# Three PSUM pools instead of two in a fused attention-and-gate kernel: own banks for attention and for the gate

## The chip, the cores and the metric

The kernel runs on one core of a Trainium2 chip. The metric is the device time of one execution in microseconds (us), lower is better. A profile is one execution taken with the hardware profiler; all times inside it are counted from the start of its span. Engines are named as the profile names them: PE (TensorE matmul), PEld (its weight load), DVE (VectorE), ACT (ScalarE), POOL (GpSimd), SP (SyncE).

On one core a run is called slow when it took over 1.5% more than the fastest run of the same kernel.

## The reference, cut to what matters

Eight batches (B = 8) of eight heads, 576 positions, head size 64. First an attention with 32 landmarks, whose middle factor is a 32 x 32 pseudo-inverse found by six Newton steps; then, on its output, a projection to three parts, a convolution over the sequence by Fourier transform of the second part, a product of the three, and an output projection.

```
A  = softmax(q k_lm^T)   Bm = softmax(q_lm k_lm^T)   C = softmax(q_lm k^T)
Z  = Bm^T / (...)
6 times: Z = 2 Z - Z Bm Z                  # the Newton steps, a serial chain
attn = A Z C v
x1, x2, x3 = split(attn @ w_proj)
y   = x1 * irfft(rfft(x2) * rfft(filter)) * x3
out = y @ w_out
```

Within a batch everything depends on what came before. Between batches nothing does, so the attention of batch b+1 can run while the gate of batch b runs, if there is room for both.

## The kernel before

The Python program is a recording: a scheduler turns it into one instruction list per engine, each executed in order. It places an instruction where its inputs are ready by its own reckoning and a buffer of the pool is free, earlier program lines first. So the pools decide not only who waits on the chip, but also the order in which PE, ACT and DVE get their work.

PSUM has eight banks. They were divided into three double tiles (`w`) that attention and gate share, and two single ones (`s`), used by attention's landmark and Newton chain and twice by the gate.

```python
    ps_w = ctx.enter_context(tc.tile_pool(name="ps_w", bufs=3, space=bass.MemoryType.PSUM))
    ps_s = ctx.enter_context(tc.tile_pool(name="ps_s", bufs=2, space=bass.MemoryType.PSUM))
    def wtile(dt=F32):
        return ps_w.tile([P, 2, 512 if dt == F32 else 1024], dt, tag="w", name="w")
    def stile(dt=F32):
        return ps_s.tile([P, 512 if dt == F32 else 1024], dt, tag="s", name="s")
    ...
        def newton(RZ, last):                      # attention, 6 times in a row
            pn = stile()
            ...                                    # 4 matmuls
            nx = sm.tile([P, 2, 160], F16, tag="RZ", name="RZ", bufs=3)
            nc.scalar.copy(nx[:, :, lo:160], pn2[:, :, lo:160])
        def turn_in(src, dst, cut):                # attention: transposes of k or q
            for t in range(2):
                pt = wtile(BF16)
                for n in range(12): turn(...)
                eng = nc.scalar.copy if t in cut else nc.vector.tensor_copy
                eng(dst[...], pt[:, :, 0:6 * R])
        def scores(src, t, dst):                   # attention: exp(q k_lm), exp(k q_lm)
            for w0 in (0, 2):
                pc = wtile()
                ...                                # 16 or 8 matmuls
                nc.scalar.activation(dst[...], pc[:R, 0:n, :], AF.Exp, bias=0.0, scale=scale)
    ...
    def gate(b, ZC, AE, AT):
        for jb in (1, 0, 2):
            pg = wtile()                           # projection -> G (ACT)
            ...
            if jb == 1:
                for g in range(2):
                    pf = wtile()                   # transform of A -> Ah (ACT)
        for e in range(2):
            px = wtile()                           # G x Ah -> X (ACT), T = X*HH, Y (DVE)
        px = stile()                               # a small rest of it -> XL (ACT)
        for jj in range(2):
            for n in range(2):
                pi = wtile()                       # inverse transform (INV, INL) -> eo (ACT)
            ...                                    # yc = sum and difference of eo (DVE)
            for n in range(2):
                for part in (0, 2):
                    px = wtile()                   # AT x G, times yc -> x, times x -> y (DVE)
        for w0 in range(2):
            po = wtile()                           # y x wout -> os (ACT) -> out
        po = stile()                               # the last 64 rows of it
    ...
    for b in range(B):
        ...
        if b + 1 < B:
            att[b + 1] = attention(b + 1)
        gate(b, *att.pop(b))
```

The softmax here doesn't subtract the row's maximum and nothing guards it: scores larger than these inputs give would overflow.

Of the kernel before, what the change touches and what calls it, by code (L numbers as in the profile page):

```python
# [8 lines left out]
F32 = mybir.dt.float32  # L9
BF16 = mybir.dt.bfloat16  # L10
F16 = mybir.dt.float16
AF = mybir.ActivationFunctionType
# [7 lines left out]
def kernel(  # L20
# [10 lines left out]
    nc = tc.nc  # L31
    B, H, S, D = q.shape
    m = 32
    blk = S // m
    Dm = H * D
    scale = 1.0 / math.sqrt(D)
    P = 128
    R = 96
    NC = S // R
    HS = S // 2  # L40
    CP = NC // 2
# [7 lines left out]
    io = ctx.enter_context(tc.tile_pool(name="io", bufs=2))  # L49
    big = ctx.enter_context(tc.tile_pool(name="big", bufs=2))  # L50
    sm = ctx.enter_context(tc.tile_pool(name="sm", bufs=2))
    ps_w = ctx.enter_context(tc.tile_pool(name="ps_w", bufs=3, space=bass.MemoryType.PSUM))
    ps_s = ctx.enter_context(tc.tile_pool(name="ps_s", bufs=2, space=bass.MemoryType.PSUM))

    def wtile(dt=F32):
        return ps_w.tile([P, 2, 512 if dt == F32 else 1024], dt, tag="w", name="w")

    def stile(dt=F32):
        return ps_s.tile([P, 512 if dt == F32 else 1024], dt, tag="s", name="s")

    def mm(o, l, r, start=True, stop=True):
        nc.tensor.matmul(o, l, r, start=start, stop=stop, skip_group_check=True)  # L62

    def turn(o, i, idn):
        nc.tensor.matmul(o, i, idn, is_transpose=True, start=True, stop=True)  # L65
# [75 lines left out]
    for i in range(2):  # L141
        t = [consts.tile([P, TW], BF16, name=f"{n}T{i}") for n in "kq"]
# [3 lines left out]
        lm = consts.tile([P, H, 2, 2, m], BF16, name=f"lm{i}")  # L146
# [4 lines left out]
    def attention(b):  # L151
        kn, qn = loaded.pop(b)
        vn = vbufs[b % NV]
        kT, qT = turned[b % 2]
        lm = lms[b % 2]
# [3 lines left out]
        for i in range(NC // 2):  # L159
            for n in range(4):  # L160
                src = kn if n < 2 else qn
                c = (2 * i + n) if n < 2 else (3 * (n - 2) + i)
# [54 lines left out]
        def newton(RZ, last):  # L217
            pn = stile()
            pn2 = pn[:, 0:320].rearrange("p (g x) -> p g x", g=2)
            lo = 128 if last else 0  # L220
            for g in range(2):
                mm(pn2[:, g, lo:160], RZ[:, g, 0:128], RZ[:, g, lo:160], stop=False)
                mm(pn2[:, g, 128:160], identh, RZ[:, g, 128:160], start=False)
            nx = sm.tile([P, 2, 160], F16, tag="RZ", name="RZ", bufs=3)
            nc.scalar.copy(nx[:, :, lo:160], pn2[:, :, lo:160])  # L225
            return nx

        def turn_in(src, dst, cut):
            flat = src.rearrange("p h c d -> p h (c d)")
            for t in range(2):  # L230
                pt = wtile(BF16)
                for n in range(12):
                    i = 12 * t + n
                    turn(pt[:, n // 6, (n % 6) * R:(n % 6) * R + R],
                         flat[:, i // CP, P * (i % CP):P * (i % CP) + P], ident[:R, :R])
                eng = nc.scalar.copy if t in cut else nc.vector.tensor_copy
                eng(dst[:, 12 * R * t:12 * R * (t + 1)].rearrange("p (a r) -> p a r", a=2),  # L237
                    pt[:, :, 0:6 * R])

        def scores(src, t, dst):  # L240
            for w0 in (0, 2):
                pc = wtile()
                cps = range(w0, min(w0 + 2, CP))
                for cp in cps:
                    pv4 = pc[:, cp - w0, :].rearrange("p (c x l) -> p c x l", c=2, l=m)
                    for h in range(H):
                        off = (h * CP + cp) * R
                        mm(pv4[:, :, 4 * (h % 2) + h // 2, :], src[:, off:off + P],
                           lm[:, h, t].rearrange("p c l -> p (c l)"))
                n = len(cps)  # L250
                nc.scalar.activation(  # L251
                    dst[:, 2 * w0:2 * w0 + 2 * n, :].rearrange("p (a c) l -> p a (c l)", a=n),
                    pc[:R, 0:n, :], AF.Exp, bias=0.0, scale=scale)

        turn_in(kn, kT, ())
        RZ = newton(RZ, False)
        eC = big.tile([R, NC, 256], BF16, tag="eC", name="eC")
        scores(kT, 0, eC)
        RZ = newton(RZ, False)
        turn_in(qn, qT, (1,))  # L260
        RZ = newton(RZ, False)
        eA = big.tile([R, NC, 256], BF16, tag="eA", name="eA")
        scores(qT, 1, eA)
        RZ = newton(RZ, False)


        pv = wtile()
        vflat = vn.rearrange("p h c d -> p (h c d)")
        for g in range(2):
            for c in range(NC):  # L270
                for x in range(4):
                    h = 2 * x + g
# [30 lines left out]
        A = big.tile([R, NC, 256], F16, tag="A", name="A")  # L303
# [5 lines left out]
        nc.vector.tensor_tensor(AE[:, 0], A[:, 0:3], A[:, 3:6], op=ALU.add)  # L309
        nc.vector.tensor_tensor(AE[:, 1], A[:, 0:3], A[:, 3:6], op=ALU.subtract)  # L310
        AT = big.tile([P, 2, S], F16, tag="AT", name="AT")
        pt = wtile(F16)
        for g in range(2):
            for c in range(NC):
                turn(pt[:, g, c * R:(c + 1) * R], A[:, c, 128 * g:128 * g + 128],
                     identh[:R, :R])
        nc.vector.tensor_copy(AT, pt[:, :, 0:S])
        return ZC, AE, AT


# [102 lines left out]
    def gate(b, ZC, AE, AT):  # L423
# [20 lines left out]
        for e in range(2):  # L444
            px = wtile()
# [8 lines left out]
            nc.vector.tensor_tensor(T, X.unsqueeze(2).to_broadcast([P, 2, 2, Dm]),  # L454
                                    HH[:, e], op=ALU.mult)
            nc.vector.tensor_tensor(Y[:, e], T[:, 0], T[:, 1], op=ALU.add)  # L456
        px = stile()
        for g in range(2):
            mm(px, Ah[:, g, 2 * P:3 * P], G[:, g, Dm:2 * Dm], start=(g == 0), stop=(g == 1))
        XL = big.tile([P, Dm], BF16, tag="XL", name="XL")  # L460
# [5 lines left out]
        for jj in range(2):  # L466
# [13 lines left out]
            for n in range(2):  # L480
                j = 2 * jj + n
                cur = yc[:, n]
                for part in (0, 2):
                    px = wtile()
# [14 lines left out]
        def store(src, i0, i1, j0, j1):  # L499
            i = i0  # L500
            while i < i1:
                c = i // R
                hi = min(i1, (c + 1) * R)
                nc.sync.dma_start(ob[c // 3, c % 3, i - c * R:hi - c * R, j0:j1],
                                  src[i - i0:hi - i0])
                i = hi

        for w0 in range(2):
            po = wtile()
# [7 lines left out]
            for n in range(2):  # L517
                i0 = P * (2 * w0 + n)
                store(os[:, n], i0, i0 + P, 0, Dm)
        po = stile()  # L520
        i0 = 4 * P
        for j in range(4):
            for n in range(2):
# [4 lines left out]
        for n in range(2):  # L528
            store(os[64 * n:64 * n + 64], i0, S, 256 * n, 256 * n + 256)

    att = {0: attention(0)}
    tables()
    filter_spectrum()
    for b in range(B):
        if b + 2 < B:
            load_qk(b + 2)
            load_v(b + 2)
# [3 lines that stand above are left out]
# [30 lines left out]
```

## Time and profile before

The time was 358.62 us, median of two runs (357.8 and 359.45); the profiled execution took 364.05 us, with a span of 362.3 us on the core.

| | before |
|---|---|
| period of one batch in the steady stretch | 41 us |
| busy per such period: PE, DVE, ACT | 32.7, 21.8, 19.2 us |
| the two gates at the end, which run alone | about 24 us each |

The page of the kernel before: busy time of each engine, then the span in 40 slices (a digit is the busy share in tenths; PEclk is the granted clock of PE in tenths).

```profile
PE 273.9 (76%) x2809; PEld 158.6 (44%) x2809; DVE 186.1 (51%) x386; ACT 163.0 (45%) x250; POOL 37.1 (10%) x77
...
PEclk9999999989969995699868995699858995699698
```

No engine is full, and the clock of PE dips to 5 or 6 tenths once in every four to five slices, that is once per batch. The same as a table of stretches (start:end and length in us; busy time and number of instructions of PE, PEld, DVE, ACT, POOL; granted clock; DMA share; GB/s), for one period of the kernel before:

```profile
core 0: us, PE busy (x) PEld busy (x) DVE busy (x) ACT busy (x) POOL busy (x), PEclk, DMA share, GB/s
181.00:188.00 7.00, 7.00 (x42) 2.69 (x37) 0.75 (x1) 4.56 (x6) 0.00 (x0) 0.50 0.18 27
188.00:192.00 4.00, 1.47 (x8) 0.47 (x7) 3.28 (x4) 2.18 (x3) 0.00 (x0) 0.93 0.00 0
192.00:196.00 4.00, 3.95 (x20) 2.49 (x19) 0.63 (x2) 1.28 (x2) 0.00 (x0) 0.64 0.00 0
196.00:218.00 22.00, 18.30 (x262) 11.66 (x262) 13.77 (x28) 10.55 (x17) 3.08 (x4) 1.00 0.48 92
218.00:222.00 4.00, 1.96 (x30) 1.38 (x28) 3.40 (x10) 0.64 (x2) 0.00 (x0) 0.60 1.46 196
```

In 218 to 222 PE is half empty: these are attention's last Newton steps, a chain between PE and ACT. The start of the gate comes next in every period (181 to 188 is the same stretch one period earlier); it looks full, but at half the clock. In 188 to 192 PE waits for DVE. The timeline of the kernel before shows the work behind this (start, length, engine, line, operation; in brackets the idle time before it and what ended it):

```profile
181.45 3.38 PE L62 MATMUL w<-F,AE 96*128 96x320 f16 x12
188.72 2.38 DVE L454 TENSOR_TENSOR T<-X,HH 128x2048 bf16<-128x2048 bf16 x2 [6.96 <-ACT X L452]
191.75 1.14 PE L62 MATMUL w<-INV,Y 128*128 128x288 f16 x4 [2.54 <-DVE Y L456]
```

Twelve AE matmuls take 3.38 us. DVE has nothing to do for 7 us before T, then PE has nothing to do for 2.5 us before INV. These holes stand in a row because nothing of the other batch is there to fill them.

### The profile page before, as it was taken

How to read it: one execution, taken by the hardware profiler on the slowest of the kernel's cores; microseconds unless marked ns; L12 is line 12 of the kernel's file. 1: busy time of each engine (PE TensorE's matmuls, PEld its weight loads, DVE VectorE, ACT ScalarE, POOL GpSimd, SP SyncE). 2: the span in 40 equal slices, each digit the busy share in tenths (PEclk: the TensorE clock that was granted, in tenths of full speed). 3: DMA queues.
4: the chain of work that ended last, by engine and by line, in shares of the span. 5: the costliest groups of instructions: out<-in, count | busy, mean ns of one | idle time of the engine just before them, and what ended most of it. 6: DMA issues, size and time to landing. Idle time of an engine off the chain costs nothing.

```text
span 362.3 us, 6617 instructions
## 1 busy us (share of the span) xinstructions
PE 273.9 (76%) x2809; PEld 158.6 (44%) x2809; DVE 186.1 (51%) x386; ACT 163.0 (45%) x250; POOL 37.1 (10%) x77
## 2 busy tenths in 40 slices
PE   1377987699596977789587977789596977789681
PEld 1165474255334553355434553355434563254350
DVE  2296446465627564475626465465626465461470
ACT  1148373525562464426471473425562373526412
POOL 8554020000200030001200020000000000000000
PEclk9999999989969995699868995699858995699698
DMA  8999978003920098004910098004000040004004
GB/s 113 207 200 206 163 96 103 0 0 72 214 45 0 22 195 113 0 2 98 214 17 0 5 205 122 0 0 117 18 0 2 0 133 2 0 2 115 16 2 130
DMA packets 33838, 26.71 MB, mean 74 GB/s; under 512 B 14160, under 2 KB 29520, under 8 KB 33808
## 3 DMA queue, kind: packets, MB, share of 16 engines
q0 software_dynamic: 27408, 16.85, 33.5%
q1 hardware_dynamic: 6400, 9.44, 9.4%
q8 instruction: 22, 0.36, 0.4%
q14 instruction: 8, 0.07, 0.1%
HBM read 33.69 MB, written 9.44 MB: 119 GB/s over the span
## 4 chain that ended last, share of the span: by engine, by line
PE 51%; DVE 19%; ACT 18%; issue 5%; DMA 3%; POOL 1%; ACTq 0%; DVEq 0%; POOLq 0%
PE w L62 36%; PE w L65 8%; PE s L62 7%; ACT RZ L225 5%; DVE T L454 4%; DVE x L494 4%; DMA filt<-in_moe_filter_fft_dram 3%; ACT eo L476 3%; ACT qT L237 2%; ACT X L452 2%; DVE yc L478 2%; ACT eA L251 2%; DVE yc L479 2%; DVE A L304 2%; DVE kT L237 1%
## 5 line engine op out<-in xcount | busy, mean ns | idle before, releaser
L62 PE MATMUL w<-AT,G 128*128 128x288 f16 x256 | 43.5, 306 | 9.5 <-DVE x L494 8.5
L454 DVE TENSOR_TENSOR T<-X,HH 128x2048 bf16<-128x2048 bf16 x16 | 19.0, 1222 | 56.9 <-ACT X L452 56.8
L476 ACT CAST eo<-w 128x576 bf16<-128x576 f32 x32 | 20.3, 639 | 61.7 <-PE w L62 55.8
L62 PE MATMUL w<-INV,Y 128*128 128x288 f16 x128 | 30.0, 343 | 22.4 <-DVE Y L456 22.3
L62 PEld LDWEIGHTS <-G 128*128 128x128 bf16 x256 | 26.7, 104 | 23.6 <-issue 14.5
L432 ACT CAST G<-w 128x1024 bf16<-128x1024 f32 x24 | 23.6, 1022 | 21.7 <-PE w L62 21.7
L62 PE MATMUL w<-wout,y 128*128 128x512 bf16 x128 | 30.4, 380 | 0.2
L62 PEld LDWEIGHTS <-Y 128*128 128x128 bf16 x128 | 14.0, 114 | 32.9 <-DVE Y L456 26.3
L62 PE MATMUL s<-RZ 128*128 128x160 f16 (+1 forms) x96 | 16.8, 243 | 13.9 <-ACT RZ L225 13.9
L225 ACT CAST RZ<-s 128x320 f16<-128x320 f32 (+1 forms) x48 | 18.7, 389 | 15.3 <-PE s L62 15.2
L62 PE MATMUL w<-F,AE 96*128 96x320 f16 x96 | 25.5, 450 | 0.0
L516 ACT COPY os<-w 128x1024 f32<-128x1024 f32 x16 | 16.2, 1012 | 19.8 <-PE w L62 19.3
L478 DVE TENSOR_TENSOR yc<-eo 128x576 bf16<-128x576 bf16 x16 | 7.3, 458 | 33.6 <-ACT eo L476 33.6
L298 DVE TENSOR_REDUCE rA<-eA 96x48 f32<-96x1536 bf16 x8 | 14.0, 1749 | 18.7 <-ACT eA L251 18.7
L494 DVE TENSOR_TENSOR x<-w,yc 128x576 bf16<-128x576 f32 x32 | 22.7, 752 | 1.7
L62 PEld LDWEIGHTS <-y 128*128 128x128 bf16 (+1 forms) x192 | 13.6, 101 | 20.9 <-issue 8.4
L494 DVE TENSOR_TENSOR y<-w,x 128x576 bf16<-128x576 f32 x32 | 22.6, 747 | 0.0
L62 PE MATMUL w<-G,Ah 128*128 128x512 bf16 x64 | 21.3, 494 | 0.2 <-ACT Ah L441 0.2
L79 POOL DMA_DIRECT2D kn<-in_k_dram x8 | 6.4, 803 | 140.2 <-PE w L65 129.2
L62 PE MATMUL w<-INL,YL 128*128 128x288 f16 x64 | 20.2, 341 | 0.0
L166 ACT CAST lmn<-s 128x512 f16<-128x512 f32 x8 | 4.7, 586 | 32.7 <-PE s L62 32.7
L62 PEld LDWEIGHTS <-RZ 128*128 128x128 f16 x96 | 9.4, 104 | 20.5 <-ACT RZ L225 19.7
(145 smaller groups left out, 489.6 us busy)
## 6 DMA issues: line engine op xcount, KB each, us to landing
kn<-in_k_dram POOLq DMA_DIRECT2D x8, 576.0 KB, 8.8
qn<-in_q_dram POOLq DMA_DIRECT2D x16, 288.0 KB, 7.5
vb<-in_v_dram POOLq DMA_DIRECT2D x8, 576.0 KB, 7.7
out_dram<-os SPq DMA_DIRECT2D x24, 192.0 KB, 2.6
out_dram<-os SPq DMA_DIRECT2D x16, 128.0 KB, 2.4
wproj<-in_moe_w_proj_dram POOLq DMA_DIRECT2D x3, 512.0 KB, 18.1
out_dram<-os SPq DMA_DIRECT2D x24, 64.0 KB, 2.0
out_dram<-osl SPq DMA_DIRECT2D x16, 64.0 KB, 3.9
```

Source lines behind the costliest of these rows:

```text
L62: nc.tensor.matmul(o, l, r, start=start, stop=stop, skip_group_check=True)
L65: nc.tensor.matmul(o, i, idn, is_transpose=True, start=True, stop=True)
L225: nc.scalar.copy(nx[:, :, lo:160], pn2[:, :, lo:160])
L237: eng(dst[:, 12 * R * t:12 * R * (t + 1)].rearrange("p (a r) -> p a r", a=2), pt[:, :, 0:6 * R])
L251: nc.scalar.activation(dst[:, 2 * w0:2 * w0 + 2 * n, :].rearrange("p (a c) l -> p a (c l)", a=n), pc[:R, 0:n, :], AF.Exp, bias=0.0, scale= ...
L298: nc.vector.tensor_reduce(rA, eA.rearrange("p c (h l) -> p (c h) l", l=m), axis=AX.X, op=ALU.add)
L432: nc.scalar.copy(G[:, :, Dm * jb:Dm * (jb + 1)], pg)
L454: nc.vector.tensor_tensor(T, X.unsqueeze(2).to_broadcast([P, 2, 2, Dm]), HH[:, e], op=ALU.mult)
L476: nc.scalar.copy(eo[:, n], pi[:, :, 0:HS])
L478: nc.vector.tensor_tensor(yc[:, :, 0], eo[:, :, 0], eo[:, :, 1], op=ALU.add)
L494: nc.vector.tensor_tensor(nx, px[:, :, 0:HS], cur, op=ALU.mult)
L516: nc.scalar.copy(os, po)
```

## The change

The intent is to give attention and gate PSUM of their own, so that neither waits for the other's tiles. Banks: two double tiles for the gate, two single ones for attention's large steps, two single ones for its small chain. To fit, the transposes and scores are cut into single-bank tiles with a copy each, and the two products of the gate that were in the small pool go to the gate's own. No arithmetic changes.

```diff
-    ps_w = ctx.enter_context(tc.tile_pool(name="ps_w", bufs=3, space=bass.MemoryType.PSUM))
+    ps_w = ctx.enter_context(tc.tile_pool(name="ps_w", bufs=2, space=bass.MemoryType.PSUM))
+    ps_a = ctx.enter_context(tc.tile_pool(name="ps_a", bufs=2, space=bass.MemoryType.PSUM))
     ps_s = ctx.enter_context(tc.tile_pool(name="ps_s", bufs=2, space=bass.MemoryType.PSUM))
+    def atile(dt=F32):
+        return ps_a.tile([P, 512 if dt == F32 else 1024], dt, tag="a", name="a")
 ...
-            for t in range(2):
-                pt = wtile(BF16)
-                for n in range(12):
+            for t in range(4):
+                pt = atile(BF16)
+                for n in range(6):
 ...                                                # one copy per tile, 576 columns
-        turn_in(qn, qT, (1,))
+        turn_in(qn, qT, (1, 3))
 ...
-            for w0 in (0, 2):
-                pc = wtile()
+            for cp in range(CP):
+                pc = atile()
 ...                                                # one exp per tile, 512 columns
-        pv = wtile()
+        pv = atile().rearrange("p (g e) -> p g e", g=2)
 ...                                                # AT transposes: one atile and copy per half
-        px = stile()
+        px = wtile()[:, 0]                         # gate, XL
 ...
-        po = stile()
+        po = wtile()[:, 0]                         # gate, last output tile
```

More of the change, by code (lines that the diff above doesn't have):

```diff
@@ L229, in turn_in @@
             flat = src.rearrange("p h c d -> p h (c d)")
-            for t in range(2):
-                pt = wtile(BF16)
-                for n in range(12):
-                    i = 12 * t + n
-                    turn(pt[:, n // 6, (n % 6) * R:(n % 6) * R + R],
+            for t in range(4):
+                pt = atile(BF16)
+                for n in range(6):
+                    i = 6 * t + n
+                    turn(pt[:, n * R:n * R + R],
                          flat[:, i // CP, P * (i % CP):P * (i % CP) + P], ident[:R, :R])
                 eng = nc.scalar.copy if t in cut else nc.vector.tensor_copy
-                eng(dst[:, 12 * R * t:12 * R * (t + 1)].rearrange("p (a r) -> p a r", a=2),
-                    pt[:, :, 0:6 * R])
+                eng(dst[:, 6 * R * t:6 * R * (t + 1)], pt[:, 0:6 * R])
         def scores(src, t, dst):
-            for w0 in (0, 2):
-                pc = wtile()
-                cps = range(w0, min(w0 + 2, CP))
-                for cp in cps:
-                    pv4 = pc[:, cp - w0, :].rearrange("p (c x l) -> p c x l", c=2, l=m)
-                    for h in range(H):
-                        off = (h * CP + cp) * R
-                        mm(pv4[:, :, 4 * (h % 2) + h // 2, :], src[:, off:off + P],
-                           lm[:, h, t].rearrange("p c l -> p (c l)"))
-                n = len(cps)
+            for cp in range(CP):
+                pc = atile()
+                pv4 = pc.rearrange("p (c x l) -> p c x l", c=2, l=m)
+                for h in range(H):
+                    off = (h * CP + cp) * R
+                    mm(pv4[:, :, 4 * (h % 2) + h // 2, :], src[:, off:off + P],
+                       lm[:, h, t].rearrange("p c l -> p (c l)"))
                 nc.scalar.activation(
-                    dst[:, 2 * w0:2 * w0 + 2 * n, :].rearrange("p (a c) l -> p a (c l)", a=n),
-                    pc[:R, 0:n, :], AF.Exp, bias=0.0, scale=scale)
+                    dst[:, 2 * cp:2 * cp + 2, :].rearrange("p c l -> p (c l)"),
+                    pc[:R], AF.Exp, bias=0.0, scale=scale)
         turn_in(kn, kT, ())
@@ L311, in attention @@
         AT = big.tile([P, 2, S], F16, tag="AT", name="AT")
-        pt = wtile(F16)
         for g in range(2):
+            pt = atile(F16)
             for c in range(NC):
-                turn(pt[:, g, c * R:(c + 1) * R], A[:, c, 128 * g:128 * g + 128],
+                turn(pt[:, c * R:(c + 1) * R], A[:, c, 128 * g:128 * g + 128],
                      identh[:R, :R])
-        nc.vector.tensor_copy(AT, pt[:, :, 0:S])
+            nc.vector.tensor_copy(AT[:, g], pt[:, 0:S])
         return ZC, AE, AT
```

## The prediction

> **What bounds the kernel now.** No engine is full: the page gives PE 76% (modelled ends), DVE 51%, ACT 45%. The timeline repeats every 41 us: first the attention of batch b+1, then the gate of batch b, one after the other on PE, because all share three double PSUM buffers. Two last gates run alone, about 25 us each. The chain of waits is PE 51%, DVE 19%, ACT 18%. PE loses time by:
>
> 1. Holes. A Newton step takes 0.9 us for 0.37 us of PE (attention, 208-222 us: 14 us); in the gate PE waits 2.6 us for X, T and Y (list of waits: T for X, 56.8 us).
> 2. A slow clock after them. Granted clock by stretches: 218-222 us 0.60, 181-188 us **0.50**, 192-196 us 0.64, 196-214 us 1.00. Twelve AE matmuls took 3.38 us there, 1.80 us in the last gate, which began warm. The Trainium skill, "TensorE: Matmul & The Clock Gate", Part 1, has the gate fall to half rate when PE was little busy; the 0.50 agrees. I estimate 5 us per period.
>
> **What changes.** No arithmetic. Banks go from 3x2+2 to 2x2+2+2, still eight. The scheduled order changes deeply: attention b+1's second half (Newton, query scores, value product) now stands inside gate b's first half, and attention b+2's first half inside gate b's INV/AT/output part.
>
> Added: smaller evacuations. An exp takes 1.02 us (1024 columns) or 0.61 (512): splitting costs 0.2 us; a DVE copy 0.757 us (1152) or 0.305 (288): about 0.15 us fixed. Per batch ACT +0.55 us on 20, DVE +0.6 on 22. Lost: the third double buffer, with which AT products ran ahead of the eo copies. New: in-order coupling. ACT takes Ah before the fifth Newton copy; DVE has rB, kT and qT between the gate's x and y products.
>
> **One new period** (estimate, walked by hand along the new order with traced durations at full clock):
> - projections, AE, Ah with Newton steps between, to the last G: 10 us, ACT nearly full;
> - gX, X, T, T, Y, to the first INV matmul: 5 us;
> - INV, eo, yc, four x/y products (0.75 us each), twice, with two buffers and attention's small DVE work between: 14.5 us;
> - output product and copies: 4 us;
> - half clock around the T/Y hole, still thinly filled: 1 us.
>
> Sum 34.5 us instead of 41. PE's own warm work is about 25 us, DVE 23, ACT 20.5, so 34.5 is bound by latency, not by an engine.
>
> **Total.** The first INV matmul comes at about 63 us instead of 71; six periods save 6 x 6.5 = 39 us; the last two gates lose 1 us. 358.6 - 8 - 39 + 1 = 312 us. Range 295 to 331 (periods of 31.5 to 37.5 us). Chances: faster 0.95, within 2% 0.03, slower 0.02.
>
> **What would show it.** A period of 33 to 36 us in the timeline; mean granted clock above 0.93 (before 0.877), AE near 1.8 us per 12; PE busy time falls though the matmuls are the same; DVE and ACT rise 5 us each; T still waits for X, x/y for AT products. The last two gates stay near 25 us with dips of the clock.
>
> **What would make it wrong.** In-order coupling worse than walked (a gate step behind a late Newton copy) gives 37 us and more; a clock that still falls to half costs +3 us per period; holes that fill better than I walked give 31 us.

## The result

The changed kernel took 306.74 us, median of two runs (305.39 and 308.09), against 358.62 us. The ratio is 0.855 (95% interval 0.837 to 0.874). Ratios here are the mean time of one kernel's fast runs over that of the other's in the same rounds, so not quite the ratio of the medians. In later rounds on another chip the changed kernel's fast runs came to 0.839 (0.834 to 0.844) of the kernel before.

The page of the changed kernel, the same lines:

```profile
PE 243.5 (80%) x2809; PEld 146.6 (48%) x2809; DVE 183.2 (60%) x418; ACT 160.7 (53%) x274; POOL 37.4 (12%) x77
...
PEclk9999999977999999999999999999999997999897
```

(PE's ends are modelled, so its share tells less than the clock and the period.) The dips of the clock are gone except near the start and in the two last gates. PE's busy time fell by 30 us with the same 2809 matmuls. DVE and ACT execute 32 and 24 instructions more in slightly less busy time.

One period of the changed kernel by stretches (first part: projection to the first INV matmul; second: to the last y; third: output products):

```profile
116.50:129.90 13.40, 11.60 (x186) 6.23 (x185) 8.57 (x16) 11.12 (x20) 2.31 (x3) 1.00 0.97 160
129.90:143.20 13.30, 11.53 (x129) 8.43 (x130) 11.63 (x29) 5.57 (x10) 0.77 (x1) 1.00 0.34 46
143.20:147.30 4.10, 4.07 (x38) 2.11 (x35) 0.96 (x4) 2.08 (x3) 0.00 (x0) 1.00 0.21 59
```

The period is 30.8 us instead of 41 (116.50 to 147.30), and the clock is full in all of it. Each of the two long parts has one engine nearly full: in the first part ACT is busy for 11.1 of 13.4 us, in the second DVE for 11.6 of 13.3 us. The timeline of the changed kernel where the kernel before had its holes:

```profile
148.75 1.18 PE L66 MATMUL w<-F,AE 96*128 96x320 f16 x6
...
149.77 0.23 PE L66 MATMUL s<-RZ 128*128 128x160 f16 x1
...
150.17 0.39 PE L66 MATMUL a<-lm,qT 128*128 128x64 bf16 x8
...
151.45 1.75 DVE L298 TENSOR_REDUCE rA<-eA 96x48 f32<-96x1536 bf16 x1 [7.29 <-ACT eA L251]
...
158.64 0.68 PE L69 MATMUL a<-ident,kn 96*128 96x96 bf16 x12
159.65 0.44 PE L66 MATMUL s<-lmsel,lmn 128*64 128x64 f16 x16 [0.32 <-ACT lmn L170]
160.75 0.66 PE L66 MATMUL w<-INV,Y 128*128 128x288 f16 x4 [0.66 <-DVE Y L456]
```

Newton steps (`s<-RZ`) and query scores (`a<-lm,qT`) of the next batch stand between the AE matmuls of the gate, and the transposes (`ident,kn`) of the batch after it stand in the hole before INV, of which 0.66 us is left. The six AE matmuls take 1.18 us, with a short pause among them: by their start times in the trace neighbours follow each other 0.14 us apart, before it was 0.27 us.

Where the time went, from the two profiles, cut at the first INV matmul of batch 0 (70.93 us before, 67.43 after) and of batch 6 (314.73 and 253.13):

| | before | after | gain |
|---|---|---|---|
| start, to INV of batch 0 | 70.9 | 67.4 | 3.5 |
| six periods | 243.8 (40.6 each) | 185.7 (30.95 each) | 58.1 |
| from INV of batch 6 to the end | 47.6 | 50.6 | -3.0 |
| span | 362.3 | 303.7 | 58.6 |

(The spans differ by 58.6 us and the medians by 51.9, mostly because the profiled execution of before took 364.05 us, 5 us more than its timed runs. Both profiles are of the kind that reaches the full PE rate late, see "The two groups of runs", so their starts can be compared.)

### The profile page after: what moved, and what is told of

It reads as the page before. It is cut to its first block, busy times and chain, and to the rows that moved or that the text cites. A ratio compares the mean times of both kernels' runs of the same rounds, so it can differ in the third digit from the quotient of the medians.

```text
span 303.7 us, 6675 instructions
## 1 busy us (share of the span) xinstructions
PE 243.5 (80%) x2809; PEld 146.6 (48%) x2809; DVE 183.2 (60%) x418; ACT 160.7 (53%) x274; POOL 37.4 (12%) x77
## 4 chain that ended last, share of the span: by engine, by line
PE 42%; ACT 24%; DVE 20%; issue 5%; DMA 4%; POOL 2%; ACTq 0%; DVEq 0%; POOLq 0%
PE w L66 30%; DVE T L454 6%; PE a L69 5%; PE s L66 5%; ACT RZ L229 5%; ACT eo L476 4%; DMA filt<-in_moe_filter_fft_dram 4%; ACT eA L251 3%; DVE x L494 3%; DVE y L494 3%; DVE Y L456 2%; ACT X L452 2%; ACT eC L251 2%; ACT Ah L441 2%; ACT qT L241 1%
## 5 line engine op out<-in xcount | busy, mean ns | idle before, releaser
L66 PE MATMUL w<-AT,G 128*128 128x288 f16 x256 | 41.5, 287 | 11.3 <-DVE x L494 7.8
L66 PE MATMUL w<-wout,y 128*128 128x512 bf16 (+1 forms) x192 | 34.7, 345 | 0.3
L66 PEld LDWEIGHTS <-G 128*128 128x128 bf16 x256 | 24.6, 98 | 21.0 <-issue 14.5
L66 PE MATMUL w<-INV,Y 128*128 128x288 f16 x128 | 27.3, 315 | 8.2 <-DVE Y L456 8.1
L494 DVE TENSOR_TENSOR y<-w,x 128x576 bf16<-128x576 f32 x32 | 24.1, 753 | 1.0
L66 PE MATMUL w<-F,AE 96*128 96x320 f16 x96 | 21.1, 316 | 0.4 <-ACT G L432 0.2
L69 PE MATMUL a<-ident,kn 96*128 96x96 bf16 x192 | 14.8, 229 | 7.6 <-DMA kn<-in_k_dram 7.5
L66 PE MATMUL w<-INL,YL 128*128 128x288 f16 x64 | 18.7, 315 | 1.4 <-DVE YL L463 1.4
L87 POOL DMA_DIRECT2D qn<-in_q_dram x16 | 12.3, 776 | 60.5 <-PE a L69 47.9
L241 DVE COPY kT<-a 128x576 bf16<-128x576 bf16 x32 | 13.6, 439 | 7.8 <-PE a L69 7.8
```

Source lines behind the costliest of these rows:

```text
L66: nc.tensor.matmul(o, l, r, start=start, stop=stop, skip_group_check=True)
L69: nc.tensor.matmul(o, i, idn, is_transpose=True, start=True, stop=True)
L87: nc.gpsimd.dma_start(qn[:, :, e].rearrange("p h c d -> p h (c d)"), q[b].rearrange("h (e p c) d -> e p h (c d)", e=2, c=NC // 2)[e])
L241: eng(dst[:, 6 * R * t:6 * R * (t + 1)], pt[:, 0:6 * R])
L494: nc.vector.tensor_tensor(nx, px[:, :, 0:HS], cur, op=ALU.mult)
```

## The experiments

All variants gave correct results. e1 to e4 ran on one chip, e5 to e8 on another, e9 to e12 on a third; each call had its own runs of the kernel before. For e1 to e4 the record calls the verdict unclear: only two of the seven runs of before were fast (354.03 and 358.37 us), so the ratios rest on these two, and the periods in the profiles are the safer comparison.

### 1. Smaller tiles in the shared pool: e1_shared_single

Attention's tiles are single banks, but come from the old shared pool. The gate's two small products (XL and the last output tile) come from it too, as in the changed kernel.

```diff
-    ps_w bufs=2; ps_a bufs=2
+    ps_w bufs=3
     def atile(dt=F32):
-        return ps_a.tile([P, 512 ...], dt, tag="a", name="a")
+        return wtile(dt)[:, 0]
```

> The attention's scores and transposes use single-bank tiles as in the changed kernel, but take them (half of a double tile) from the old shared pool of three; the gate's two small products sit in that pool too. Theory (own pools free the order): PE still works through attention and gate one after the other, period 37 to 41 us, time 335 to 360 us, clock still dips below 0.7 in parts of the period. Rival (the smaller tiles by themselves give the overlap): time within 3% of 306.7 us.

Measured: 350.75 us (4 runs, 347.35 to 351.83), 0.970 of before (0.953 to 0.987). The period in its profile is 38.0 us (98.60 to 136.60) with a mean clock of 0.90, and twelve AE matmuls again take 3.38 us:

```profile
98.60:136.60 38.00, 29.56 (x348) 18.12 (x349) 22.15 (x47) 18.86 (x33) 3.07 (x4) 0.90 0.48 80
```

So smaller tiles without an own pool give about 3% in time, and 2.6 of the 9.8 us that a period lost. The scheduled order fits this: the gate of a batch still stands in one piece, with nothing between its steps but the landmark matmuls of the next batch, B and B's powers (which use the small pool), and Newton steps, scores and value product come after it.

### 2. The own pool without smaller tiles: e2_split_double

Attention has one double tile of its own and keeps its old tile sizes and copies. The gate's two small products are in the gate's pool, as in the changed kernel; this is not written in the cut below.

```diff
     ps_w bufs=2
-    ps_a bufs=2, [P, 512]
+    ps_a bufs=1, [P, 2, 512]        # turn_in, scores, pv, AT as in the kernel before
```

> Own pool for attention, but as one double-bank tile with the old tile sizes and copies. Theory (own pools free the order, size is secondary): attention and gate interleave, clock near 1.00 in the steady stretch, period 31 to 33 us, time 305 to 320 us. Rival (single-bank tiles, two in flight, are needed): attention steps wait for their one tile, time 330 us or more.

Measured: 312.98 us (311.11 to 314.83), 0.867 of before (0.853 to 0.881); period 30.95 us in the profile (INV of successive batches at 106.74 and 137.69) with the clock at 1.00:

```profile
137.69:168.65 30.96, 27.39 (x346) 16.77 (x348) 20.97 (x44) 18.56 (x29) 3.07 (x4) 1.00 0.57 97
```

So the own pool, together with the move of the gate's two small products, brings nearly all of the gain; what that move is worth in it, experiment 3 shows. The single-bank tiles add at most some 2% on top, if anything, since the interval of this ratio overlaps that of the changed kernel. In the profiles they hardly shorten the steady period (30.79 to 30.80 us in the changed kernel); the difference lies in the first one, from INV of batch 0 to INV of batch 1 (39.69 us here, 31.74 in the changed kernel). Why was not looked into.

### 3. The last part of the change undone: e3_rest_in_s, then e5_px_in_s and e6_po_in_s

```diff
-        px = wtile()[:, 0]      # XL           e3 and e5
+        px = stile()
-        po = wtile()[:, 0]      # last output  e3 and e6
+        po = stile()
```

> The changed kernel with only its last part undone: the gate's XL product and the last output tile go back to the small pool that attention's chain uses. Theory: a minor part, the interleaving stays, time 304 to 316 us. Rival: these two tiles tie the attention's chain to the gate, time 322 us or more.

Measured: 327.75 us (327.06 to 334.51), 0.907 of before (0.878 to 0.937). My theory fell: two small tiles in the wrong pool take back over a third of the gain. The scheduled order gave a suspect, so the two were put back one at a time.

> The changed kernel with only the gate's XL product put back into the small pool. It lives there for about 1 us per period, and the scheduled order of PE stays that of the changed kernel almost everywhere. Theory (the output tile alone did the harm in e3_rest_in_s): time 303 to 312 us, period 30.5 to 31.5 us. Rival (both share the harm): 312 to 322 us.

> The changed kernel with only the last output tile put back into the small pool. Its first products are issued as soon as the first quarter of y is there and it keeps one of the two banks until the last quarter, so attention's landmark chain (landmarks, B, its powers) has one bank for that time; the scheduled order shows that chain behind the output products. Theory: as e3_rest_in_s, 322 to 334 us, period 35 to 36.5 us. Rival: 306 to 318 us.

Measured: e5 301.89 us (299.49 to 304.56, period 30.35 us), e6 333.53 us (328.44 to 334.06, mean of six periods 35.7 us). These rounds had one run of before that was much faster than its six others, so no ratio was formed; their median of before is 364.07 us. The output tile alone did the harm, and the XL product is, if anything, better off in the small pool. The timeline of e6 shows how:

```profile
132.96 1.14 PE L66 MATMUL w<-INV,Y 128*128 128x288 f16 x4
...
140.90 0.30 PE L66 MATMUL s<-wout,y 128*64 128x256 bf16 x2
141.13 0.39 PE L66 MATMUL s<-kn,poolk 96*32 96x512 bf16 x1
...
143.67 0.30 PE L66 MATMUL s<-wout,y 128*64 128x256 bf16 x2
147.05 0.30 PE L66 MATMUL s<-wout,y 128*64 128x256 bf16 x2
151.15 0.30 PE L66 MATMUL s<-wout,y 128*64 128x256 bf16 x2
151.38 0.22 PE L66 MATMUL s<-lm 128*32 128x32 bf16 x8
```

The tile sums over four quarters of y. Its first product is issued when the first quarter is there (140.90) and its last when the last one is (151.15): for 10.3 us it holds one of the two small banks. Attention's matmul B (`s<-lm`), which needs a bank of that pool, comes directly after, 18.4 us after the first INV matmul. In the changed kernel it is 2.0 us:

```profile
123.76 0.39 PE L66 MATMUL s<-kn,poolk 96*32 96x512 bf16 x2
...
129.96 0.66 PE L66 MATMUL w<-INV,Y 128*128 128x288 f16 x4 [0.66 <-DVE Y L456]
...
131.97 0.23 PE L66 MATMUL s<-lm 128*32 128x32 bf16 x8
```

The late B pushes the Newton steps and the key scores back, the interleaving gets thinner (the clock in INV's stretch, 132.7 to 139.7, is 0.60 again), and the period is 5 us longer.

The time for which the tile holds its bank is not the main part of this, though. B stands at the end of the landmark chain, which starts with `s<-kn,poolk`. In e6 this first matmul stands directly behind the first product of the output tile, 8.2 us after INV; in the changed kernel it stands 6.2 us before INV. That is 14.4 of the 16.4 us by which B is later. From there to B it takes 10.3 us in e6 and 8.2 us in the changed kernel. The same order is in all five kernels that keep the output tile in the small pool (before, e3, e4, e6, e7), here the kernel before:

```profile
201.44 0.41 PE L62 MATMUL s<-wout,y 128*64 128x256 bf16 x4
201.78 0.39 PE L62 MATMUL s<-kn,poolk 96*32 96x512 bf16 x2
```

So in these orders the chain of a later batch queues behind the opening of the gate's tile in the same pool. Why the scheduler queues it there (perhaps because a pool hands out its tiles in program order) was not tested.

### 4. The slow clock by itself: e4_before_warm

The kernel before in its old pools and almost its old order, with idle matmuls in the holes. Their result is not read.

```diff
+    def warm(n):
+        d = wtile()
+        for i in range(n):
+            mm(d[:, i % 2, :], ident, wproj[:, 0, 0:512])
     # if b >= 2: newton: + warm(2)     before pz: + warm(2)     before the A transposes: + warm(4)
     # gate, after the XL product: + warm(8), in every batch
```

> The kernel before, in its old order and pools, with matmuls whose result nobody reads put into the holes (after the Newton steps, around the A transposes, and while the gate waits for Y), so that PE stays busy. Theory (slow clock costs about 4 us per period): granted clock over 0.95 through the gate, twelve AE matmuls near 1.8 us instead of 3.38, time 328 to 342 us; the rest of the gain to 306.7 is overlap. Rival (the slow stretch is hidden behind ACT and DVE, and all gain is overlap): clock rises, time stays above 350 us.

Measured: 332.45 us (331.5 to 333.21), 0.921 of before (0.908 to 0.933). Its windows, from the AE matmuls to INV, to the output, and to the next AE matmuls:

```profile
94.60:103.00 8.40, 6.47 (x54) 3.00 (x47) 3.86 (x6) 6.45 (x8) 0.00 (x0) 1.00 0.35 52
103.00:119.00 16.00, 14.55 (x136) 8.72 (x138) 9.10 (x16) 5.70 (x9) 0.00 (x0) 1.00 0.06 16
119.00:131.40 12.40, 11.29 (x192) 7.20 (x193) 8.70 (x25) 6.71 (x13) 3.07 (x4) 1.00 1.19 191
```

and one line of its timeline:

```profile
94.64 1.82 PE L62 MATMUL w<-F,AE 96*128 96x320 f16 x12
```

The clock is full everywhere, the AE matmuls take 1.82 us, and the period is 36.7 us (INV at 102.99 and 139.71). PE executes more matmuls and the kernel is faster. So of the 9.8 us that a period lost (40.6 to 30.8), 3.9 us can be had by the clock alone; the other 5.9 us, by subtraction, need the overlap.

### 5. The third buffer: e7_before_two

```diff
-    ps_w bufs=3
+    ps_w bufs=2        # kernel before, nothing else
```

> The kernel before with two shared double tiles instead of three and nothing else: what the lost third buffer costs. The order stays serial (attention, then gate). Theory (third buffer worth little): 350 to 366 us, the two last gates about 1 to 1.5 us longer each than before. Rival (third buffer matters): 372 us or more.

Measured: 392.11 us (389.36 to 394.09), 8% above the median of before in the same rounds (364.07); period 44.4 us (INV at 208.72 and 253.10), mean clock of the run 0.80. I had this wrong: shared, the third buffer was worth 28 us. (Six of the seven runs of before carry the slow state; against the one fast run, 350.99 us, it is 41 us, and between the two profiles 30 us.) The experiment is not a clean measure of the buffer, though, because the scheduler's order changed with it: the last output tile is now issued early, as in e6, and holds its small bank. What it does show is that the changed kernel is not faster because two double buffers are enough for the old arrangement; they aren't.

The price of the two buffers in the changed kernel can be read from its end, where gates 6 and 7 run alone. From one gate's first INV matmul to the next one's it took 26.95 us (253.13 to 280.08), before 24.45 us (314.73 to 339.18). INV to the output products grew from 11.35 to 12.67 us, the output products from 4.13 to 4.94 us, and the rest from 8.97 to 9.34 us. In e7 the same gate takes 27.00 us (341.84 to 368.84), so two buffers cost the same without the new pools.

### 6. Who sets the length of the period: e8_ah_dve and e10_px_bal

```diff
 # e8
-                    nc.scalar.copy(Ah[:, g]...)
+                    eng = nc.vector.tensor_copy if g else nc.scalar.copy
+                    eng(Ah[:, g]...)
 # e10: e8, XL in the small pool, and
-        turn_in(kn, kT, ())
+        turn_in(kn, kT, (1, 3))
-        turn_in(qn, qT, (1, 3))
+        turn_in(qn, qT, (1,))
```

> The changed kernel with one of the gate's two Ah copies on DVE instead of ACT. In the first 13.4 us of its period ACT is busy 11.1 us while DVE waits 7.3 us in one piece. Theory (ACT's queue sets the length of this first part): the first part shrinks by 0.5 to 1.2 us, period 29.6 to 30.3 us, time 299 to 304 us. Rival (the Newton chain's latency sets it): period 30.6 us or more.

Measured: 302.3 us (297.55 to 304.29). The windows of e8:

```profile
172.50:185.30 12.80, 11.36 (x188) 6.30 (x186) 9.12 (x17) 10.77 (x20) 2.31 (x3) 1.00 1.00 169
185.30:198.60 13.30, 11.50 (x128) 8.40 (x129) 11.63 (x30) 5.57 (x10) 0.00 (x0) 1.00 0.01 1
198.60:202.70 4.10, 4.10 (x38) 2.12 (x35) 0.99 (x4) 2.05 (x3) 0.00 (x0) 1.00 0.20 57
```

Only the first part moved, from 13.4 to 12.8 us, by about the one Ah copy (0.70 us) that left ACT; the other parts are as before. ACT's queue does set the first part.

> The changed kernel with the XL product in the small pool, one Ah copy on DVE, two of four kT copies moved from DVE to ACT and the last qT copy from ACT to DVE. Theory (the first part of the period is set by ACT's queue, the second by DVE's, 11.6 of 13.3 us busy there): both parts shrink, the second by 0.5 us or more, period 28.8 to 29.7 us, time 289 to 297 us. Rival (the second part is set by the gate's own chain INV, eo, yc, x, y): the second part stays, period 29.8 to 30.3 us, time 297 to 301 us.

Measured: 306.29 us (304.91 to 309.19), 0.854 of before (0.850 to 0.857), so slower than the changed kernel itself in the same rounds (0.839). The part that I had a theory for shrank, though by less than expected: from INV to the main run of output products it took 13.0 us in one batch (194.77 to 207.80) and 12.7 in the next (225.02 to 237.74), where e8 has 13.27 (185.38 to 198.65). But moving four copies also made the scheduler move the query scores, and the rest of the period grew to 17.2 us (207.80 to 225.02), from 16.9 in e8 (its period of 30.16 less 13.27). The period is 30.1 us, no better than e8's 30.2. And the kernel lost 5.6 us in its first two batches: INV of batch 1 is at 104.80 us, where the changed kernel has 99.17 with an equally late clock (see below). Why the new order starts so badly was not settled. The ratio also compares different starts in part: the profile of e10 starts late, and its runs (304.91 to 309.19 us) lie around the slow runs of the changed kernel (305.29 to 307.9 us), which 0.839 leaves out. Between the two late profiles the spans are 304.7 and 303.7 us.

### 7. The clock in the last gates, and a version that beats both: e9 to e12

Here the idle matmuls are products of Ah and G, so that they can't be scheduled before the hole.

```diff
 # e11: changed kernel, XL in the small pool, one Ah copy on DVE, and in the gate after the XL product
+        if b >= B - 2:
+            d = atile()
+            for _ in range(9):
+                mm(d, Ah[:, 0, 0:P], G[:, 0, Dm:2 * Dm])
 # e12: the same lines in e10
```

> The changed kernel itself again, on the chip of the next three runs, for comparison: 302 to 310 us, period 30.8 us in the profile.

> The changed kernel with the XL product in the small pool, one Ah copy on DVE, and nine idle products of Ah and G (512 columns each, result not read) in the hole before INV in the two last gates, which run alone. Theory (the clock falls to half after that hole and the INV and first AT products pay for it): clock 0.95 or more from the first INV product of these gates on, each of the two gates 1 to 1.8 us shorter, time 293 to 299 us. Rival (these stretches are set by ACT and DVE): clock full, gates less than 0.5 us shorter, time about 300 us.

> The two kernels above joined: 2 to 4 us below e10_px_bal, 286 to 295 us, if their effects add.

Measured: e9 (the changed kernel again) 303.96 us over six runs, 0.839 of before by its three fast runs; e11 300.09 us over six runs, 0.818 (0.815 to 0.820) by its two fast runs, 293.5 and 293.41 us; e12 304.03 us, 0.848 (0.846 to 0.851), 2.3 us below e10.

e11 beats both kernels, by 2.5% against the changed one when fast runs are compared (two runs of e11, three of e9) and by 1.3% when all runs are. Its profile is of a slow run that starts late; between the late profiles it is 298.2 against 303.7 us. In it the clock is full in the last gates; from the last gate's first INV matmul to its output products it took 11.45 us (275.92 to 287.37), in the changed kernel 12.77 us (280.08 to 292.85). From gate 6 to gate 7 it took 26.2 instead of 26.95 us. That is 0.8 to 1.3 us per gate, around the lower end of the 1 to 1.8 us that I expected, and it contains the effect of the Ah copy and of XL as well. The clean pair is e10 and e12, which differ by the idle matmuls alone: from INV of batch 6 to the end it took 49.76 and 48.04 us, so they are worth 1.7 us for both gates together. The effects of e10 did not add.

### The two groups of runs

The six runs of e9 fall into 299.45, 300.2, 302.63 and 305.29, 305.53, 307.9 us. Its profile is of the first group (span 298.5); the changed kernel's first profile looks like the second (span 303.7). The same six matmuls of the filter's transform, in the same place of the same instruction list, from the timeline of the changed kernel's first profile:

```profile
38.65 2.74 PE L66 MATMUL w<-fs,F 96*128 96x512 f16 x6
```

and from the timeline of e9:

```profile
37.59 1.47 PE L66 MATMUL w<-fs,F 96*128 96x512 f16 x6
```

In the one profile PE stays at about half its rate until some 52 us, in the other until some 36 us. The first INV matmul follows at 67.43 and at 62.22 us, a difference of 5.2 us, which is the whole difference of the two spans. The kernel before was late as well (five of these matmuls took 2.33 us). That the other runs of a group started in the same way is not shown.

## Why the prediction was right, point by point

- **Time.** Predicted 312 us (295 to 331), measured 306.74 us. Right, but in part by luck. The measured period of 30.8 us lies below the 33 to 36 us that were to show the theory, and below the 31.5 to 37.5 us that belong to the range; six periods gained 58.1 us, where 39 were forecast. Three misses the other way took back 12 of these 19 us: the start gained 3.5 us instead of 8, the last gates lost 3.0 instead of 1, and the profile of before took 5.4 us more than the 358.6 us from which the forecast was subtracted. What happened in the period is the case that the prediction names at its end, holes that fill better than walked.
- **What bounds the kernel before** (serial phases, holes, and a clock that the holes pull down). Confirmed: the order and the pools by e1 and e2, the clock by e4. The clock's share of a period was estimated as 5 us with 1 us left over; e4 measures 3.9 us.
- **What the change does** (interleaving of two batches on PE). Confirmed by the timeline and by e2. "Perfetto Trace Analysis" in the Trainium skill, section Optimization Strategy, says of kernels whose busiest engine changes over time that "performance may be improved by interleaving those regimes"; here it took the period from 40.6 to 30.8 us. The same section says that a gap that repeats can mean that a pool of PSUM has run out; the gap of 2.5 us before INV repeats in the periods of the kernel before, and with the new pools 0.66 us of it is left.
- **The sum for one period**, 34.5 us against a measured 30.8: the mechanism was right and the size was off by four small terms that all went the same way. Projections to the last G: predicted 10 us, measured 8.7 (147.30 to 155.98). From there to INV: 5 and 4.8. INV to the last y: 14.5 and 13.2. Output: 4 and 4.1. Half clock: 1 and 0. A likely reason is the walk with the traced mean durations: an engine with a full queue is faster than the sum of them. Two G copies in a row took 1.93 us in the timeline where the mean of one is 1.026, two eo copies 1.18 where it is 0.640:

```profile
154.05 1.93 ACT L432 CAST G<-w 128x1024 bf16<-128x1024 f32 x2
...
162.39 1.18 ACT L476 CAST eo<-w 128x576 bf16<-128x576 f32 x2 [2.79 <-PE w L66]
```

The Trainium skill ("Perfetto Trace Analysis", section Optimizing Scalar/DVE Operations) says that half of the fixed part of a profiled instruction, the write acknowledgement, "overlaps with the next instruction"; the pairs agree, with 0.10 to 0.12 us less than twice the mean. Added up over the trace, the durations of the ACT instructions that start in the first part come to 12.85 us and cover 11.00 us, those of DVE in the second part come to 13.03 us and cover 11.32 us. These overlaps of 1.85 and 1.71 us are enough for the two misses of 1.3 us. That they are their cause is not shown: not every overlap need lie on the path that sets the length.

- **"DVE and ACT rise 5 us each."** Wrong for the busy time: it fell, from 186.1 to 183.2 and from 163.0 to 160.7 us. Each split does cost something (kT copies: 12.1 us in 16, now 13.6 in 32), and the durations of all instructions added up did rise, by 3.7 us on DVE (203.5 to 207.2) and by 6.3 us on ACT (172.5 to 178.7), which is near the forecast. But in the fuller queue more of the windows overlap (DVE 17.4 us before, 24.0 after; ACT 9.5 and 18.0), and in the busy time overlapped time counts once.
- **The start** was predicted to gain 8 us and gained 3.5 in the first profile and 8.7 in e9's. The 8.7 us sets an early start of the changed kernel against a late one of before; late against late it is 3.5, so the size was too large. I did not know that the start varies.
- **The last two gates** were predicted to lose 1 us and lost 3.0, of which 2.5 us lie between the INV matmuls of gates 6 and 7. The third buffer was mis-sized here and, by far, in e7.
- **Clock.** Mean 0.972, predicted above 0.93. (Both means count a stretch at the start as full in which PE ran at half its rate, see above and below.)
- **Not foreseen:** that the last line of the diff, the output tile, which I had not costed at all, decides over a third of the gain (e6).

The two things together explain the size: of the 58 us that six periods gained in the profiles, about 23 us (six times 3.9) can be had by the clock alone and about 35 us (six times 5.9) take the overlap; the last gates give 3 us back and the start adds 3.5.

## What to carry to other kernels

When the phases of two iterations could overlap but share a pool, the pool's size is not the question; the scheduled order is, so compare it before and after, and look for a tile that shares a pool with a serial chain of another iteration, so that the chain is queued behind it. Count a stretch of half clock as part of the cost of the hole that precedes it: idle matmuls in the hole tell how much that is, and in the last gates they were even worth keeping. When walking an order by hand, use the length of a pair of queued instructions, not twice the mean of one.

## What the Trainium skill lacked or had wrong

- "TensorE: Matmul & The Clock Gate", Part 1, has the clock rise after about 3.4 us of sustained work, varying by 0.5 us from run to run, and puts the whole ramp below 1% of a typical kernel. Here the same instruction list came up at some 36 us in one execution and some 52 us in another, although PE was modelled as busy for 11.92 us of the 12 us from 40 to 52; it cost 5.2 us of 304, or 1.7%. A warning on the page tells of a gate seen stuck at a quarter for over 50 us, so a long slow stretch as such is not new to it. What decides it was not tested.
- The same Part 1 warns that the clock events of a trace have been observed to be unreliable and should be cross-checked. What it lacks is a case in which the reading is too high: the granted clock read 1.00 in 36 to 52 us of the changed kernel's first profile, where six matmuls took 2.74 instead of 1.47 us. The durations of a known matmul are the safer sign.
- "PSUM — Partial Sum Buffer" tells who may touch a bank, and that banks should be emptied promptly, but not that two chains of work that share a pool of its tiles can end up one behind the other: with the gate's output tile in attention's small pool (e6), attention's landmark matmuls stand 8.2 us after INV instead of 6.2 us before it, and the period is 5 us longer.
- "Perfetto Trace Analysis", section Optimizing Scalar/DVE Operations, suggests breaking up instructions that cause bubbles on other engines. It leaves out where the pieces come from: in a shared pool the smaller pieces gave 3% here (e1), while an own pool without smaller pieces gave 13% (e2; in both the gate's two small products had been moved).
